# Thirteen GpSimd operations on a tile of their own in the end part of an attention and gMLP kernel

## The chip, the cores and the metric

The kernel runs on one core of a Trainium2 chip. The metric is the device time of one execution in microseconds. A core has five engines that run beside each other, each in the order of its own instructions: TensorE (PE, matmuls), VectorE (DVE), ScalarE (ACT), GpSimd (POOL) and SyncE (SP, which here only issues DMAs).

## The reference, cut to what matters

Attention with a threshold over 8 batches of 8 heads, 576 positions and 64 columns a head, followed by a gated MLP with a spatial projection (gMLP) over each batch. All inputs and the output are fp32.

```python
scores = q @ k.T / 8
scores = where(scores >= max(scores) - tau, scores, -1e9)
attn = exp(scores - max(scores)); attn /= sum(attn)
x = attn @ v                              # (8, 576, 512), the heads side by side
h = maximum(x @ w_in, 0)                  # (8, 576, 1024)
u, v = h[..., :512], h[..., 512:]
v_n = (v - mean(v)) / sqrt(var(v) + 1e-6)
v_s = w_spatial @ v_n + b_spatial         # over the 576 positions
out = (u * v_s) @ w_out                   # (8, 576, 512)
```

## The kernel before, in words

**Tiling.** The 64 heads go in 32 pairs. A pair has 576 rows of scores, four blocks of 128 and a rest of 64; the rests of two pairs share a block, so there are 144 steps. A step makes scores on PE (L830), their maximum on DVE (L859), a shift on POOL or DVE (L873, L869), the masked exponentials on ACT and DVE (L887, L890, L925, L909, L918), a transpose of the numerators by DMA (L930) and the product with v on PE (L505, L510), whose result DVE divides by the sums (L545, L548). When a batch has its x, the gMLP follows in blocks of 128 rows or columns: v (L641, L656), its norm (L675 to L708), u (L723, L728), the spatial product (L752, L757), the gate (L766, L769) and the output (L781, L792).

**The order.** It is written out by hand. ORDER holds one list of short tokens for each batch and `run_token` (L1111) turns a token into the instructions of one piece of work; nothing is reordered afterwards, so the order of the program is the order of each engine's own queue. A tile that one engine writes and another reads makes the reader wait; an instruction that waits holds up everything behind it on its engine.

**The end part.** After the eight lists comes LAST (L165), four short lists. LAST[1] ends the attention of the last two pairs and the output of batch 6; its last instructions on DVE and ACT are copies of output blocks (L792). Then `last_gmlp` (L941) does the gMLP of batch 7, in four parts between `yield`s:
- Part 1: 16 products for v (L955), the relu with ACT (L981, L984), the statistics on DVE (L961, L962). For chunk 3 ACT takes the sum, POOL makes the negative mean from it (L991) and ACT the squares (L995). POOL makes the reciprocal roots with a power: chunks 0 to 2 at once, chunks 3 and 4 later (both L965). The rest of v and the rest of batch 6's output are one bank (L641, L644), of which ACT takes one half here (L989).
- LAST[2]: u blocks 0 to 2 on PE (L723), which ACT evicts (L426).
- Part 2: shifts on DVE (L1004, L1007, L1012) and the norms, written to `vn`: chunks 0, 1 and 4 on DVE, 2 on POOL (all L970), 3 on ACT (L1010).
- LAST[3]: u block 3 and the rest of u (L723, L728).
- Part 3: ACT copies the other half of that bank (L1017), PE makes the spatial products (L1027: first the column blocks 0 and 1, chunk by chunk, then 2 and 3; then the rest, L1038), DVE gates (L1031, L1041), PE makes the output (L1048, L1059), ACT and DVE copy it out (L1050, L1064) and SP sends it (L1051, L1066); block 1 is sent by POOL's queue and one half of the rest by ACT's. The fourth part is empty.

PSUM has eight banks, which are used in turn, so a matmul can have to wait until the reader of a bank's former content is done. The third and fourth of the spatial products' banks had held L1017's half and the first block of u.

Of the kernel before, what the change touches and what calls it, by code (L numbers as in the profile page):

```python
# [9 lines left out]
F32 = mybir.dt.float32  # L10
# [5 lines left out]
ALU = mybir.AluOpType  # L16
# [172 lines left out]
def kernel(  # L189
# [17 lines left out]
    nc = tc.nc  # L207
    B, H, S, D = q.shape
# [5 lines left out]
    P = 128  # L214
    const = ctx.enter_context(tc.tile_pool(name="const", bufs=1))
# [28 lines left out]

    mhalf = const.tile([P, 1], F32, name="mhalf")
    zero = const.tile([P, 1], F32, name="zero")
    raised = const.tile([P, 2, 2], F32, name="raised")
    warm = const.tile([P, P], BF16, name="warm")

# [556 lines left out]
    def way(g):  # L806

        return WAYS[min(g // 18, len(WAYS) - 1)][g % 18]
# [34 lines left out]
    def turn_bank(g, eng):  # L843

        turned[g] = eng.nop()
        follow(turned[g], opened[g])
# [7 lines left out]
    def top(g, heads=slice(0, 2)):  # L854

        if g not in peak:
            peak[g] = small.tile([P, 2], F32, name="peak")
        for h in range(heads.start, heads.stop):
            nc.vector.tensor_tensor_reduce(  # L859
                out=e_ring[g % 3][:, h, :], in0=view(s_ring[g % 2], at[h], [[1, S]]),  # L860
                in1=zero.broadcast_to([P, S]), scale=1.0, scalar=float("-inf"),
                op0=ALU.add, op1=ALU.max, accum_out=peak[g][:, h:h + 1])

    def shift(g, engine):

        nm = negm[g] = small.tile([P, 2], F32, name="negm")
        down = -(scale if steps[g][1] == 4 else 1.0)
        if engine is nc.vector:
            engine.scalar_tensor_tensor(out=nm, in0=peak[g], scalar=down,  # L869
                                        in1=raised[:, 0 if way(g) == "a" else 1, :],  # L870
                                        op0=ALU.mult, op1=ALU.add)
        else:
            engine.tensor_scalar(out=nm, in0=peak[g], scalar1=down,  # L873
                                 scalar2=float(tau) + (0.0 if way(g) == "a" else half_step),
                                 op0=ALU.mult, op1=ALU.add)
# [6 lines left out]
    def spread(g, h):  # L882

        s = e_ring[g % 3][:, h, :]
        e, bias_ = e_ring[g % 3][:, h, :], negm[g][:, h:h + 1]
        if way(g) in "nrs":
            nc.scalar.activation(out=half_e(g)[0][:, h, :], in_=s, func=ACT.Exp,  # L887
                                 bias=bias_, scale=scale if steps[g][1] == 4 else 1.0)
        elif on_act(g):
            nc.scalar.activation(out=e, in_=s, func=ACT.Prelu, bias=bias_,  # L890
                                 scale=scale if steps[g][1] == 4 else 1.0, alpha=1e30)
        else:
            nc.scalar.activation(out=e, in_=s, func=ACT.Exp, bias=bias_)
# [217 lines left out]
    def run_token(tok, it):  # L1111

        name, _, d = tok.partition(":")
        on_vector[0] = name[0] == "d"
        name = name[on_vector[0]:]
        relay = nc.gpsimd
        if name[0] in "agv" and name[1] in "GB":
            relay = {"a": nc.scalar, "g": nc.gpsimd, "v": nc.vector}[name[0]]
            name = name[1:]
        b = it - int(d or 0)  # L1120
        if (name, b) in done or b < 0:
            return
        kind = name.rstrip("0123456789")
        a = [int(x) for x in name[len(kind):]] if kind not in "SGYMHKBEFZWCAT" else []
        g = 18 * b + int(name[len(kind):]) if kind in "SGYMHKBEFZWCAT" else 0
        if b >= B or g >= len(steps):
            return
        if kind in stepwise and way(g) not in stepwise[kind]:
            return
        i = 4 * b + a[0] if a else 0  # L1130
        m = 2 * b + a[0] if a else 0
        if kind in "SGYMHKEFBZWCAT":
            {"S": scores, "G": lambda g: turn_bank(g, relay), "Y": scores_end, "M": top, "E": lambda g: spread(g, 0),
             "F": lambda g: spread(g, 1), "H": lambda g: top(g, slice(0, 1)),
             "K": lambda g: top(g, slice(1, 2)), "B": lambda g: shift(g, relay), "Z": exps, "W": mask, "C": keep, "A": pick, "T": turn_p}[kind](g)
        elif kind in ("QA", "QB", "qa", "qb"):
            task("q", i, kind[1] in "Bb")[1 + (kind[0] == "q")]()
        elif kind in ("QR", "qr", "kd"):
            task("r", i)[1 + ("QR", "qr", "kd").index(kind)]()
        elif name == "sk1":  # L1140
            shape_qk(1, (1,))
        elif kind in ("sq", "sv"):
            (shape_qk if kind == "sq" else shape_v)(i)
        elif kind == "P":
            task("p", m, a[1])[0](a[2])
        elif kind in ("i", "p"):
            task("p", m, a[1])[1 + (kind == "p")]()
        elif kind in ("XP", "xp"):
            task("x", i, i == NPAIR - 1)[1 + (kind == "xp")]()
        elif kind in ("RP", "rp"):  # L1150
            task("t", m, a[1])[1 + (kind == "rp")]()
        elif kind in ("WS", "ws"):
            task("w", a[0])[1 + (kind == "ws")]()
        elif kind in ("X", "XR"):
            send_x(m, 4 if kind == "XR" or 2 * m in x_on_pe else 0, 5 if kind == "XR" else 9)
        elif kind == "L":
            load_of[b][a[0]]()
        elif kind[0] == "C":
            chores[kind[:2]][len(kind) == 3](a[0])
        elif kind == "OUT":  # L1160
            task("o", b, a[0])[3]() if a[0] < 4 else task("v", b + 1, 4)[6]()
        elif kind == "bv":
            task("v", b, a[0])[2](False)
        elif kind == "bs":
            task("v", b, a[0])[7]()
        elif kind == "ba":
            task("v", b, a[0])[8]()
        elif kind in ("n", "k", "N"):
            task("v", b, a[0])[3 + "nkN".index(kind)]()
        else:  # L1170
            task(kind[-1], b, a[0])[1 + (kind[0] == "e")]()
        done.add((name, b))
        on_vector[0] = False

    Z = B - 1
    with tc.manual_schedule():
        nc.vector.memset(warm, 1.0)
        for w in (1, 0):
            for h in range(2):
                load_first(w, h, (nc.sync, nc.scalar)[h])  # L1180
        for w in (0, 1):
            load_rest(0, w, 0, 2)()
        make_identity(nc, identf)
        clear()
        nc.vector.memset(zero, 0.0)
        nc.gpsimd.memset(raised[:, 0], float(tau))
        nc.gpsimd.memset(raised[:, 1], float(tau) + half_step)
        nc.vector.memset(ntau, -float(tau))
        nc.vector.memset(mhalf, -0.5)
        nc.scalar.activation(out=ctau, in_=ntau, func=ACT.Exp)  # L1190
        nc.vector.tensor_copy(out=identb, in_=identf)
        nc.vector.tensor_copy(out=identh, in_=identf)
        for w in (0, 1):
            load(1, 1, w)()
            load_rest(0, w, 2)()
        load(0, 2, 2)()
        for w in (2, 3):
            load_rest(0, w)()
        for _ in range(8):
            nc.tensor.matmul(out=next_bank().rearrange(  # L1200
                "p (a b) -> p a b", a=4), lhsT=warm,
                rhs=warm.unsqueeze(1).broadcast_to([P, 4, P]), start=True, stop=True)
        shape_first()
        first()
        clear_vn()
        shape_qk(1, (0,))
        load_of = [group_loads((b, 0)) + group_loads((b, 1)) for b in range(B)]
        for it in range(B):
            for tok in ORDER[min(it, len(ORDER) - 1)].split():
                run_token(tok, it)  # L1210

        for tok in LAST[0].split():
            run_token(tok, B)
        inner.close()
        wide.append(ctx.enter_context(tc.tile_pool(name="ps_t", bufs=6, space=PSUM,
                                                  reuse_waits="tile")))
        for tok in LAST[1].split():
            run_token(tok, B)
        rest = last_gmlp(Z)
        next(rest)  # L1220
        for tok in LAST[2].split():
            run_token(tok, B)
        next(rest)
        for tok in LAST[3].split():
            run_token(tok, B)
        next(rest)
        next(rest, None)


# [33 lines left out]
```

## Time and profile before

| | |
|---|---|
| Median of the runs | 429.72 us (2 runs, 429.71 to 429.73) |
| The profiled execution, its own time | 429.39 us |
| Its span in the profile | 427.6 us |
| Granted TensorE clock | 1.0 |
| Busy: PE, DVE, ACT, POOL | 405.0, 384.0, 386.1, 191.4 us |
| Traffic with HBM | 32.79 MB read, 9.44 MB written |

Times in the profile are microseconds from the start of the span. A row of the timeline gives the start, the duration, the engine, the line, the operation, what it writes and reads with shapes, and in brackets the idle time of the engine ahead of it and what ended that. Consecutive rows of the same kind are merged, with their number behind an x. A group row gives the number, the summed busy time and the mean in ns. PEld is TensorE's weight load, an engine name with a small q its instruction queue.

### The profile page before, as it was taken

What the parts mean: (1) busy time and instruction counts of PE and PEld (TensorE: products, weight loads), DVE (VectorE), ACT (ScalarE), POOL (GpSimd) and SP (SyncE); (2) the same over time, 40 slices, a digit from 0 to 9 for tenths busy, and PEclk for the clock granted to TensorE, in tenths of its full rate; (3) what the DMA queues carried; (4) which work ended last, traced back from release to release, by engine and by line L of the source; (5) the groups of instructions that cost most, each with busy time, mean ns of one, the idle gap of its engine ahead of it and who ended that gap; (6) DMA issues with size and microseconds to landing.
All of it is one profiled execution on the core that took longest, in us unless ns stands there. A gap on an engine that the chain in (4) does not pass through costs nothing.

```text
span 427.6 us, 13266 instructions
## 1 busy us (share of the span) xinstructions
PE 405.0 (95%) x4978; PEld 253.3 (59%) x5029; DVE 384.0 (90%) x1035; ACT 386.1 (90%) x567; POOL 191.4 (45%) x469
## 2 busy tenths in 40 slices
PE   8778978999999999999999999999999999999995
PEld 4456655566555675575665657656665666565642
DVE  6999989999899899989999999989999989999562
ACT  4999979999999999999999999999999999999362
POOL 2566437763246633554235631374233753255020
PEclk9999999999999999999999999999999999999999
DMA  7999999999999999998999989999989999989913
GB/s 196 288 280 182 263 273 227 168 182 195 239 265 171 214 213 188 204 210 227 214 165 280 211 165 252 217 221 210 236 138 229 228 214 206 160 150 214 180 57 117
DMA packets 224703, 88.18 MB, mean 206 GB/s; under 512 B 195648, under 2 KB 220352, under 8 KB 224640
## 3 DMA queue, kind: packets, MB, share of 16 engines
q1 hardware_dynamic: 224192, 86.75, 102.3%
q8 instruction: 39, 0.64, 0.6%
q10 hardware_dynamic: 368, 0.33, 0.2%
q0 software_dynamic: 80, 0.26, 0.2%
q14 instruction: 24, 0.20, 0.2%
HBM read 32.79 MB, written 9.44 MB: 99 GB/s over the span
## 4 chain that ended last, share of the span: by engine, by line
PE 62%; DVE 11%; ACT 9%; DMA 7%; issue 5%; POOL 3%; SPq 1%; POOLq 0%; DVEq 0%; ACTq 0%
PE s L830 25%; DVE e L859 7%; PE f L752 6%; DMA pT<-p 6%; PE f L448 5%; PE f L510 5%; PE f L723 4%; PE f L656 4%; ACT e L890 3%; PE f L781 3%; ACT e L887 2%; PE f L505 2%; ACT p L925 1%; DMA xT<-xn 1%; PE f L641 1%
## 5 line engine op out<-in xcount | busy, mean ns | idle before, releaser
L859 DVE CUSTOM_DVE_ANT_0 e<-s,zero 128x576 f32<-128x576 f32 x288 | 204.3, 752 | 5.8 <-PE s L830 1.4
L830 PE MATMUL s<-qkT 64*64 64x160 f32 (+1 forms) x2304 | 172.9, 413 | 4.5 <-DVE peak L859 3.7
L890 ACT ACTIVATE e<-e,negm 128x576 f32<-128x576 f32 x204 | 148.3, 766 | 4.8 <-PE s L830 2.3
L830 PEld LDWEIGHTS s<-qkT 64*64 64x64 f32 x2304 | 105.3, 132 | 53.2 <-issue 19.1
L925 ACT ACTIVATE p<-e 128x1152 f16<-128x1152 f32 x102 | 117.1, 1157 | 0.8
L873 POOL TENSOR_SCALAR negm<-peak 128x2 f32<-128x2 f32 x93 | 21.5, 231 | 133.3 <-DVE peak L859 89.7
L887 ACT ACTIVATE e<-e,negm 128x576 f16<-128x576 f32 x84 | 62.4, 767 | 2.0 <-POOL negm L873 1.3
L510 PE MATMUL f<-v,pT 128*128 128x65 bf16 x984 | 44.6, 194 | 0.0
L510 PEld LDWEIGHTS <-pT 128*128 128x128 f16 x1024 | 41.9, 98 | 2.4 <-issue 0.6
L918 DVE TENSOR_TENSOR p<-e 128x576 int32<-128x576 int32 x42 | 34.4, 822 | 0.5
L752 PE MATMUL f<-wsT,vn 128*128 128x512 bf16 x121 | 31.9, 380 | 0.9 <-DVE qkT L424 0.2
L505 PE MATMUL f<-v,pT 128*128 128x130 bf16 x123 | 27.2, 221 | 4.0 <-DMA pT<-p 3.9
L333 POOL CAST v<-vl 128x512 bf16<-128x512 f32 x32 | 21.3, 666 | 18.6 <-PE s L830 17.5
L708 POOL TENSOR_SCALAR vn<-vrel,rs,nm 128x512 bf16<-128x512 f32 (+1 forms) x35 | 27.9, 798 | 3.6
L723 PE MATMUL f<-xT,w_in 128*128 128x512 bf16 x102 | 28.5, 380 | 1.0 <-ACT qkT L430 0.3
L656 PE MATMUL f<-w_in,xT 128*128 128x512 bf16 x98 | 27.0, 380 | 1.4 <-DMA xT<-xn 0.3
L548 DVE TENSOR_TENSOR xn<-f,r 128x384 bf16<-128x384 f32 x46 | 25.2, 554 | 0.7
L781 PE MATMUL f<-w_o,gT 128*128 128x512 bf16 x94 | 25.1, 379 | 0.4
L859 DVE DVE_READ_ACCUMULATOR2_ANT peak<- 128x1 f32 x288 | 23.9, 83 | 0.0
L306 POOL COPY qn<-ql 128x512 f32<-128x512 f32 x31 | 19.7, 636 | 5.9 <-DMA ql<-in_q_dram 2.7
L752 PEld LDWEIGHTS <-vn 128*128 128x128 bf16 x140 | 12.8, 98 | 15.5 <-issue 3.1
L448 PE MATMUL f<-identf,kn 128*128 128x128 f32 x124 | 19.8, 282 | 2.2 <-DVE qkT L424 1.5
(175 smaller groups left out, 560.2 us busy)
## 6 DMA issues: line engine op xcount, KB each, us to landing
vl<-in_v_dram SPq DMA_DIRECT2D x16, 512.0 KB, 5.2
ql<-in_q_dram SPq DMA_DIRECT2D x15, 512.0 KB, 5.5
kl<-in_k_dram SPq DMA_DIRECT2D x15, 512.0 KB, 5.7
out_dram<-oo SPq DMA_DIRECT2D x12, 512.0 KB, 4.2
pT<-p SPq DMA_TRANSPOSE x141, 4.4
uT<-in_moe_w_in_dram SPq DMA_DIRECT2D x3, 512.0 KB, 6.4
uT<-in_moe_w_spatial_dram SPq DMA_DIRECT2D x2, 576.0 KB, 6.8
vx<-in_v_dram SPq DMA_DIRECT2D x16, 64.0 KB, 3.8
```

Of the source, the lines that this page charges most:

```text
L448: nc.tensor.transpose(out=t[:, c * P:(c + 1) * P], in_=nat[i][which][:, c, :], identity=identf)
L505: nc.tensor.matmul(out=t[:, at:at + 130], lhsT=pt[:, 4, rows], rhs=vt[:, 4:6, :].rearrange("p b d -> p (b d)"), start=True, stop=False)
L510: nc.tensor.matmul(out=t[:, at + 65 * h:at + 65 * h + 65], lhsT=pt[:, 5 * h + j, rows], rhs=vt[:, 6 * h + j, :], start=False, stop=(h == 1 ...
L656: nc.tensor.matmul(out=t, lhsT=x_of(b, f, slice(c * P, (c + 1) * P)), rhs=w_in[:, f, 512:1024], start=(f == 0), stop=(f == 3))
L723: nc.tensor.matmul(out=t, lhsT=w_in[:, m, f * P:(f + 1) * P], rhs=x_of(b, m, slice(0, 512)), start=(m == 0), stop=(m == 3))
L752: nc.tensor.matmul(out=t, lhsT=vn[:, c, f * P:(f + 1) * P], rhs=wsT[:, c, 0:512], start=(c == 0), stop=(c == 4))
L781: nc.tensor.matmul(out=t[:n], lhsT=gs[b][:, f, c * P:c * P + n], rhs=w_o[:, f, :], start=(f == 0), stop=(f == 3))
L830: made.append(nc.tensor.matmul(out=s_ring[g % 2][halves[k], at[h] + lo:at[h] + hi], lhsT=qks[n][halves[h], 0, m:m + 64], rhs=qks[n][halves ...
L859: nc.vector.tensor_tensor_reduce(out=e_ring[g % 3][:, h, :], in0=view(s_ring[g % 2], at[h], [[1, S]]), in1=zero.broadcast_to([P, S]), scal ...
L887: nc.scalar.activation(out=half_e(g)[0][:, h, :], in_=s, func=ACT.Exp, bias=bias_, scale=scale if steps[g][1] == 4 else 1.0)
L890: nc.scalar.activation(out=e, in_=s, func=ACT.Prelu, bias=bias_, scale=scale if steps[g][1] == 4 else 1.0, alpha=1e30)
L925: nc.scalar.activation(out=numerators(g), in_=e_ring[g % 3].rearrange("p h s -> p (h s)"), func=ACT.Exp)
```

## The change

Two tiles are added, a column of ones and a tile `trial` of 128x576 fp32. DVE fills the column at the start, and `trial` after LAST[1]. Nine operations on POOL follow, ahead of `last_gmlp`, and four more behind its third part. Each reads `trial` and writes it in place; scalars are numbers or the columns `zero` and `one`. One of the thirteen is a tensor_tensor with the column `zero` repeated over the free dimension, the others are tensor_scalar with one or two operations. Nothing else reads `trial`.

```diff
@@ -244,6 +244,8 @@
     mhalf = const.tile([P, 1], F32, name="mhalf")
     zero = const.tile([P, 1], F32, name="zero")
+    one = const.tile([P, 1], F32, name="one")
+    trial = const.tile([P, S], F32, name="trial")
     raised = const.tile([P, 2, 2], F32, name="raised")
@@ -1183,6 +1185,7 @@
         nc.vector.memset(zero, 0.0)
+        nc.vector.memset(one, 1.0)
@@ -1216,6 +1219,16 @@
         for tok in LAST[1].split():
             run_token(tok, B)
+        nc.vector.memset(trial, 2.0 ** -6)
+        nc.gpsimd.tensor_scalar(out=trial, in0=trial, scalar1=zero, scalar2=2.0 ** -3, op0=ALU.subtract, op1=ALU.mult)
+        nc.gpsimd.tensor_scalar(out=trial, in0=trial, scalar1=zero, scalar2=2.0 ** -3, op0=ALU.add, op1=ALU.mult)
+        nc.gpsimd.tensor_scalar(out=trial, in0=trial, scalar1=one, scalar2=zero, op0=ALU.mult, op1=ALU.add)
+        nc.gpsimd.tensor_scalar(out=trial, in0=trial, scalar1=zero, scalar2=None, op0=ALU.subtract)
+        nc.gpsimd.tensor_scalar(out=trial, in0=trial, scalar1=2.0 ** -120, scalar2=None, op0=ALU.mult)
+        nc.gpsimd.tensor_scalar(out=trial, in0=trial, scalar1=one, scalar2=zero, op0=ALU.mult, op1=ALU.add)
+        nc.gpsimd.tensor_tensor(out=trial, in0=trial, in1=zero.broadcast_to([P, S]), op=ALU.subtract)
+        nc.gpsimd.tensor_scalar(out=trial, in0=trial, scalar1=zero, scalar2=one, op0=ALU.add, op1=ALU.mult)
+        nc.gpsimd.tensor_scalar(out=trial, in0=trial, scalar1=one, scalar2=None, op0=ALU.mult)
         rest = last_gmlp(Z)
         next(rest)
         for tok in LAST[2].split():
@@ -1224,6 +1237,10 @@
         for tok in LAST[3].split():
             run_token(tok, B)
         next(rest)
+        nc.gpsimd.tensor_scalar(out=trial, in0=trial, scalar1=zero, scalar2=one, op0=ALU.subtract, op1=ALU.mult)
+        nc.gpsimd.tensor_scalar(out=trial, in0=trial, scalar1=2.0, scalar2=zero, op0=ALU.mult, op1=ALU.add)
+        nc.gpsimd.tensor_scalar(out=trial, in0=trial, scalar1=zero, scalar2=2.0, op0=ALU.is_ge, op1=ALU.mult)
+        nc.gpsimd.tensor_scalar(out=trial, in0=trial, scalar1=zero, scalar2=None, op0=ALU.add)
         next(rest, None)
```

## The prediction

> **What bounds the kernel now.** The page of the profile comes first: TensorE, VectorE and ScalarE are busy for 90% or more of the span, GpSimd (POOL) for less than half, and in the last tenth of the span POOL is nearly empty.
>
> ```profile
> span 427.6 us, 13266 instructions
> PE 405.0 (95%) x4978; PEld 253.3 (59%) x5029; DVE 384.0 (90%) x1035; ACT 386.1 (90%) x567; POOL 191.4 (45%) x469
> POOL 2566437763246633554235631374233753255020
> ```
>
> A share over the whole span says nothing of a stage, so the chain of work that ended last, cut to the last 35 us, is next. It runs over TensorE without a gap: products for the last batch (L955), ends and u (L641, L723, L728), the spatial products (L1027, L1038), the output products (L1048, L1059).
>
> ```profile
> 413.64 0.47 PE t L728 x16
> 414.11 2.16 PE t L1027 x10
> 416.26 2.16 PE f L1027 x10
> 418.42 0.58 PE t L1038 x20
> ...
> 423.01 0.05 PE f L1059
> ```
>
> So PE sets the end, and POOL's results cost nothing as long as they stand ready when PE comes to them. How much they have to spare is in the timeline of the same stage (start, duration, engine, line, operation, in brackets the idle time before it).
>
> ```profile
> 405.70 0.68 DVE L792 COPY vl<-f 128x512 f32<-128x512 f32 x1
> 406.34 0.06 DVE L948 MEMSET var<- 128x5 f32 x1
> 408.47 0.69 DVE L961 BATCH_NORM_STATS2 st<-vrel 128x6 f32<-128x512 f32 x1 [2.05 <-ACT vrel L981]
> 410.15 0.19 POOL L991 TENSOR_SCALAR nmean<-sm 128x1 f32<-128x1 f32 x1 [15.82 <-ACT vrel L984]
> 410.62 0.71 ACT L995 ACTIVATE sq<-vrel,nmean 128x512 bf16<-128x512 f32 x1
> 411.23 0.19 ACT L995 ACTIVATION_READ_ACCUMULATOR sq<-vrel,nmean 128x1 f32 x1
> 411.26 0.87 POOL L965 TENSOR_TENSOR rstd<-var,mhalf 128x3 f32<-128x3 f32 x1 [0.92 <-DVE var L985]
> 411.32 0.58 ACT L426 ACTIVATE uT<-f 128x512 bf16<-128x512 f32 x1
> 411.95 0.60 ACT L426 ACTIVATE uT<-t 128x512 bf16<-128x512 f32 x1
> 412.07 0.14 DVE L1000 TENSOR_SCALAR var<-ss 128x1 f32<-128x1 f32 x1
> 412.16 0.16 DVE L1004 SCALAR_TENSOR_TENSOR shift<-mvs,rstd 128x3 f32<-128x3 f32 x1
> 412.29 0.70 POOL L965 TENSOR_TENSOR rstd<-var,mhalf 128x2 f32<-128x2 f32 x1 [0.16 <-DVE var L1000]
> 412.36 0.55 DVE L970 TENSOR_SCALAR vn<-vrel,rstd,shift 128x512 bf16<-128x512 f32 x1
> 412.99 0.77 POOL L970 TENSOR_SCALAR vn<-vrel,rstd,shift 128x512 bf16<-128x512 f32 x1
> 413.10 0.94 DVE L970 TENSOR_SCALAR vn<-vrel,rstd,shift 128x512 bf16<-128x512 f32 x1
> 413.31 0.80 ACT L1010 ACTIVATE vn<-vrel,shift,rstd 128x512 bf16<-128x512 f32 x1
> 414.12 0.54 DVE L970 TENSOR_SCALAR vn<-o,rstd,shift 64x512 bf16<-64x512 f32 x1
> 414.88 0.58 ACT L1017 COPY kl<-f 64x512 f32<-64x512 f32 x1
> 421.65 0.78 POOL L1051 DMA_DIRECT2D out_dram<-ql  x1 [7.90 <-ACT ql L1050]
> ```
>
> POOL has two idle stretches here: 15.82 us before L991 and 7.90 us before its one DMA. But the first ends in the norms of the last batch, and these run POOL, ACT, DVE, POOL, DVE, PE in turn. Chunk 0 of vn is ready at 412.91 and PE turns to L1027 at 414.11; chunk 1 is ready at 414.04 and is wanted at 414.54. The spare time is about a microsecond at most.
>
> **The change, part by part.** Nothing is removed and nothing is moved. Added are a memset of a 128x1 column at the start, a memset of the 128x576 tile on DVE, nine operations on POOL behind it, and four more on POOL behind the output stage.
>
> The small memset (128x1) costs DVE no more than the five columns of L948, 0.06 us; DVE waits for the first loads behind it, which hides it, and without that cover it costs the 0.06. Taken as 0.
>
> The large memset stands in DVE's order behind the copy of 405.70, which ends at 406.38. Its price comes from two memsets of other sizes:
>
> ```profile
> L269 DVE MEMSET vn<- 64x512 bf16 x2 | 1.0, 485 | 0.2 <-issue 0.2
> L1177 DVE MEMSET warm<- 128x128 bf16 x1 | 0.2, 165 | 0.8 <-PEq L1244 0.8
> ```
>
> That is (485 - 165) / 384 = 0.83 ns for an element and 0.54 us for 576. On DVE it lies in the 2.05 us of idle time before L961; uncovered it would cost 0.54. On POOL it matters at once, because the first operation waits for it: 406.38 + 0.54 + 0.08 for the handover gives 407.00. So of POOL's 15.82 us of idle time only the last 3.15 can be used: the operations start 12.6 us after the idle time does.
>
> The nine operations work in place, each on the result of the one before. All but one are TENSOR_SCALAR, one is TENSOR_TENSOR with a repeated column. No row has this size or these combinations, so the nearest rows of POOL are these (first two lines: one source line with its minimum, median and maximum; then groups with a mean; then two copies in time order):
>
> ```profile
> L708 POOL TENSOR_SCALAR vn<-vrel,rs,nm x35: 761/767/1202, 77.3 to 389.4; 128x512 bf16<-128x512 f32 x28, 64x512 bf16<-64x512 f32 x7
> L703 POOL TENSOR_SCALAR nm<-mv,rs x28: 252/259/585, 76.9 to 389.0; 128x1 f32<-128x1 f32 x22, 64x1 f32<-64x1 f32 x6
> ...
> L394 POOL TENSOR_TENSOR bias<-bias,wsb 128x5 f32<-128x5 f32 x2 | 0.4, 198 | 0.2
> ...
> 100.54 0.61 POOL L306 COPY qn<-ql 128x512 f32<-128x512 f32 x1
> 101.10 0.61 POOL L306 COPY kn<-kl 128x512 f32<-128x512 f32 x1
> ...
> 389.02 0.26 POOL L703 TENSOR_SCALAR nm<-mv,rs 128x1 f32<-128x1 f32 x1
> 389.38 0.77 POOL L708 TENSOR_SCALAR vn<-vrel,rs,nm 128x512 bf16<-128x512 f32 x1
> ```
>
> From 259 ns for one column and 767 for 512 follows 0.99 ns an element, so 0.83 us for 576; a dependent operation follows 0.10 behind the one before it (389.28 to 389.38). That makes 0.93 from start to start. The low end is a plain copy, 0.56 from start to start, 0.63 at 576. The high end is L708's slowest, 1.20, which at 576 with the gap is 1.45. I take 0.93 for each of the eight, because L708 is the same kind of instruction. The TENSOR_TENSOR took 0.198 at five columns (L394), against 0.19 for one column (L991; 0.185 within its rounding), so at most 3.3 ns an element: its price lies between 0.63 (as the copy) and an estimated 2.1 (0.19 + 1.9 at 576, and the gap). I take 1.4, the middle. Sum: 8 x 0.93 + 1.4 = 8.84 us, and the ninth ends at T = 415.84; with the low prices (9 x 0.63) at 412.7, with the high ones (8 x 1.45 + 2.1) at 420.7.
>
> Who is queued behind them: L991, both L965, POOL's L970 and POOL's DMA L1051, all in POOL's order. L991 would have started at 410.15 and now starts at T + 0.1. What follows, with the durations above:
> - L991 ends at T + 0.29. ACT's square starts at T + 0.33 and its sum is read at T + 1.13 (0.80 as from 410.62 to 411.42). Queued behind the square on ACT are three evictions of u, and behind these L1010 (vn chunk 3).
> - POOL's first L965 runs from T + 0.39 to T + 1.26, beside the square. DVE's L1000 stands ahead of L1004 in DVE's order, so DVE comes to the shifts at T + 1.36, and chunk 0 is written at T + 2.1.
> - The second L965 ends at T + 2.12; DVE's chunk 1 is ready at T + 3.2 and chunk 4 at T + 3.8, at the distances that they have behind it now.
> - ACT: 0.70 to the first eviction, 3 x 0.63 for the evictions (two of them waited for PE before, now all three are ready), then L1010 at T + 2.92, and from there 2.15 to the end of L1017 (413.31 to 415.46): T + 5.07.
> - PE: chunk 1 at T + 3.2 and four chunks of 0.43 end the first ten of L1027 at T + 4.9. The next ten write the bank that L1017 reads, so they start at T + 5.10, where they started at 416.26. Everything behind that moves as one.
>
> The end is late by T + 5.10 - 416.26 = T - 411.16. For T = 415.84 that is **4.7 us**. The low prices give 1.5, the high ones 9.5; nothing in the edit takes work away, so below nothing is excluded.
>
> The last four operations follow POOL's DMA. On the old time scale that DMA issue ends at 422.43, and four of 0.93 end at about 426.2. The end then waits for the last output DMA:
>
> ```profile
> out_dram<-ql ACTq DMA_DIRECT2D x1, 64.0 KB, 2.8
> ...
> 423.55 0.55 ACTq L1066 DMA_DIRECT2D out_dram<-ql  x1
> ```
>
> It lands at 423.55 + 2.8 = 426.35. The four are hidden, with some 0.15 us to spare; at 1.45 each they end at 428.3 and cost 1.9. I take 0.
>
> Sum: the profiled execution took 429.39 (span 427.6), and with 4.7 it takes 434.1; the runs shown lie 0.33 above that execution (429.72), so 434.4.
>
> **The rivals.**
> *Everything is hidden: not slower.* The break-even is T = 411.16, so nine operations in 4.16 us, 0.46 us each. That needs POOL to stream these forms faster than its plain copy (0.63 at this size); no row does. The time would be 429.7. The same time would come out if the dead results made the operations vanish, for which I see no reason.
> [...]
>
> *TensorE's clock falls.* By the working above PE has nothing to do from 414.11 to about 418.0 (T + 2.1), 3.9 us. The one place where the granted clock fell is the end of the span (columns: window, its length, busy time of five engines, granted clock, DMA share, GB/s):
>
> ```profile
> 427.20:427.40 0.20, 0.00 (x0) 0.00 (x0) 0.00 (x0) 0.00 (x0) 0.00 (x0) 1.00 0.00 0
> 427.40:427.60 0.20, 0.00 (x0) 0.00 (x0) 0.00 (x0) 0.00 (x0) 0.00 (x0) 0.60 0.00 0
> ```
>
> That is 4.3 us after the last matmul (423.06). 3.9 is just short of it, which speaks against a fall here. If it fell to 0.60, the 8.5 us of PE work still open (6.8 from 416.26 to 423.06, and 1.7 of the first ten) would take up to 5.7 more; with about half of it at that clock, 2.9: 437.3.
> [...]
>
> *Some form is far dearer than L708.* POOL's power took 0.87 for three columns and 0.70 for two (L965), 0.17 a column, so single operations can be slow by orders. Against it: the added ones only add, subtract, multiply and compare. If three of the first nine took 3 us, T and the end move by 6.2: 440.6.
>
> *The last four set the end*, at 1.45 each: 434.4 + 1.9 = 436.3.
>
> **How the numbers follow.** Forecast 0.57; last four 0.12; clock 0.12; a dear form 0.12; all hidden 0.07. The range goes from the low prices, 429.7 + 1.5 = 431.2, to the high ones, 429.7 + 9.5 = 439.2; that leaves out the hidden case and most of the dear form. A difference of 2% is 8.6 us, about what a measurement of this kernel can tell from no change: 438.3 is passed by most of the dear forms and by a part of the clock case, 0.13 together; faster by 2% needs work to disappear, 0.01; within, 0.86.
>
> **What would show it.** In the profile after: the memset on DVE at about 406.4, POOL's first added operation near 407.0, the ninth ending near 415.8, L991 right behind it; ACT's wait ahead of L995 and PE's wait ahead of L1027 (near 4 us, put down to vn) in place of none; the second ten of L1027 behind L1017; the last four under the landing of the last DMA. The chain would pass over POOL. It is wrong if L991 keeps its 410.15, if PE does not wait ahead of L1027, if PE's clock drops there, or if the last instruction of POOL ends the span.

## The result, and the profile after

The changed kernel takes 443.23 us (442.58 to 443.87, 2 runs) against 429.72, a ratio of 1.0314 with a 95% interval of 1.025 to 1.0379: slower by over 2%, and above the range. The forecast was 434.4. The profiled execution took 443.87 with a span of 442.0, which is 14.4 more than the span of before.

The first view is the timeline of POOL in the changed kernel (start, duration, line, shapes, idle time before; the lines of the old code stand two or more higher than before: L991 is now L993, L965 L967, L970 L972, L1010 L1012, L1017 L1019, L1027 L1029).

```profile
408.06 2.22 POOL L1223 TENSOR_SCALAR trial<-trial,zero 128x576 f32<-128x576 f32 x1 [12.79 <-DVE mvs L951]
410.38 0.74 POOL L1224 TENSOR_SCALAR trial<-trial,zero 128x576 f32<-128x576 f32 x1
411.22 0.82 POOL L1225 TENSOR_SCALAR trial<-trial,one,zero 128x576 f32<-128x576 f32 x1
412.13 1.73 POOL L1226 TENSOR_SCALAR trial<-trial,zero 128x576 f32<-128x576 f32 x1
413.95 1.66 POOL L1227 TENSOR_SCALAR trial<-trial 128x576 f32<-128x576 f32 x1
415.71 0.82 POOL L1228 TENSOR_SCALAR trial<-trial,one,zero 128x576 f32<-128x576 f32 x1
416.61 1.15 POOL L1229 TENSOR_TENSOR trial<-trial,zero 128x576 f32<-128x576 f32 x1
417.87 0.81 POOL L1230 TENSOR_SCALAR trial<-trial,zero,one 128x576 f32<-128x576 f32 x1
418.78 1.72 POOL L1231 TENSOR_SCALAR trial<-trial,one 128x576 f32<-128x576 f32 x1
420.46 0.19 POOL L993 TENSOR_SCALAR nmean<-sm 128x1 f32<-128x1 f32 x1
...
433.79 2.29 POOL L1240 TENSOR_SCALAR trial<-trial,zero,one 128x576 f32<-128x576 f32 x1
436.19 0.74 POOL L1241 TENSOR_SCALAR trial<-trial,zero 128x576 f32<-128x576 f32 x1
437.04 2.21 POOL L1242 TENSOR_SCALAR trial<-trial,zero 128x576 f32<-128x576 f32 x1
439.35 1.74 POOL L1243 TENSOR_SCALAR trial<-trial,zero 128x576 f32<-128x576 f32 x1
```

Operations of one size and one opcode (TENSOR_SCALAR) cost between 0.74 and 2.29 us. Then the chain of work that ended last, which now passes over POOL:

```profile
418.78 1.72 POOL trial L1231
420.50 0.17 POOL nmean L993
...
423.58 3.58 PE t L1029 x8
427.17 2.52 PE f L1029 x10
429.69 0.58 PE t L1040 x20
```

And the busy time in stretches of the end part (length; PE, PEld, DVE, ACT, POOL busy; granted clock; DMA share; GB/s):

```profile
415.00:422.40 7.40, 0.00 (x1) 0.01 (x1) 0.77 (x3) 1.71 (x5) 6.74 (x8) 0.67 0.00 0
422.40:427.17 4.77, 4.63 (x11) 1.46 (x12) 1.92 (x5) 2.60 (x6) 0.84 (x2) 0.50 0.13 27
...
417.40:417.60 0.20, 0.00 (x0) 0.00 (x0) 0.00 (x0) 0.00 (x0) 0.20 (x1) 0.84 0.00 0
417.60:417.80 0.20, 0.00 (x0) 0.00 (x0) 0.00 (x0) 0.00 (x0) 0.15 (x1) 0.50 0.00 0
...
427.60:427.80 0.20, 0.20 (x2) 0.00 (x0) 0.20 (x1) 0.00 (x0) 0.00 (x0) 0.56 0.00 0
427.80:428.00 0.20, 0.20 (x2) 0.10 (x1) 0.20 (x1) 0.00 (x0) 0.00 (x0) 1.00 0.00 0
```

PE has nothing to do for 7.4 us, its clock falls to half in that time and stays there for the first half of the spatial products. The 14.4 us of the span come apart as follows:
- **0.9** lie ahead of the end part: DVE's copy of 405.70 now starts at 406.60. Run e8 below shows no such cost of the two tiles, and in e5, the same kernel once more, the first of the nine starts at 407.17 and not at 408.06, so it is scatter between executions.
- **8.15** are the nine (by working out): the first ten of L1029 would have ended at 423.58 + 8 x 0.216 = 425.31 at full clock, where they ended at 416.26 + 0.9.
- **2.2** are the clock: these eight took 3.58 in place of 1.73, and the ten behind them 2.52 in place of 2.16.
- **3.1** are the last four: from the last DMA issue to the end it is 442.0 - 434.81 = 7.19, and it was 427.6 - 423.55 = 4.05. The waits of SP's queue at the end (us in total, times, longest) are for the last output DMA, as before (2.3 there too), and for POOL's last operation:

```profile
SPq L1275 <- POOL trial L1243: 3.1, 1, 3.1
SPq L1275 <- DMA out_dram<-ql: 2.3, 1, 2.3
```

### The profile page after: what moved, and what is told of

It is laid out like the page before. It is cut to its first block, busy times and chain, and to the rows that moved or that the text cites. A ratio compares the mean times of both kernels' runs of the same rounds, so it can differ in the third digit from the quotient of the medians.

```text
span 442.0 us, 13332 instructions
## 1 busy us (share of the span) xinstructions
PE 412.1 (93%) x5029; PEld 254.3 (58%) x5029; DVE 384.5 (87%) x1037; ACT 385.7 (87%) x567; POOL 210.3 (48%) x482
## 4 chain that ended last, share of the span: by engine, by line
PE 63%; DVE 11%; POOL 7%; ACT 6%; DMA 6%; issue 5%; POOLq 0%; SPq 0%; DVEq 0%; ACTq 0%
PE s L832 25%; DVE e L861 7%; PE f L754 6%; PE f L512 5%; PE f L450 5%; PE f L725 5%; DMA pT<-p 4%; PE f L658 4%; PE f L783 3%; ACT e L892 2%; PE f L507 2%; DMA xT<-xn 1%; PE f L469 1%; ACT p L927 1%; ACT e L889 1%
## 5 line engine op out<-in xcount | busy, mean ns | idle before, releaser
L920 DVE TENSOR_TENSOR p<-e 128x576 int32<-128x576 int32 x42 | 34.3, 821 | 0.4
L754 PE MATMUL f<-wsT,vn 128*128 128x512 bf16 x135 | 32.8, 380 | 0.2 <-DVE qkT L426 0.2
L725 PE MATMUL f<-xT,w_in 128*128 128x512 bf16 x116 | 29.4, 380 | 0.4 <-ACT qkT L432 0.3
L658 PE MATMUL f<-w_in,xT 128*128 128x512 bf16 x112 | 28.1, 380 | 0.5 <-DVE qkT L426 0.2
```

Of the source, the lines that this page charges most:

```text
L658: nc.tensor.matmul(out=t, lhsT=x_of(b, f, slice(c * P, (c + 1) * P)), rhs=w_in[:, f, 512:1024], start=(f == 0), stop=(f == 3))
L725: nc.tensor.matmul(out=t, lhsT=w_in[:, m, f * P:(f + 1) * P], rhs=x_of(b, m, slice(0, 512)), start=(m == 0), stop=(m == 3))
L754: nc.tensor.matmul(out=t, lhsT=vn[:, c, f * P:(f + 1) * P], rhs=wsT[:, c, 0:512], start=(c == 0), stop=(c == 4))
```

## The experiments

The theory: POOL's price for a tensor_scalar goes by its operations, some pairs are fast and all else is slow; the nine then hold up the norms, the idle time lowers PE's clock, and the last four set the end. The rivals: the slow ones are slow by circumstance (first after a pause, other engines at work), or by the values that they work on; the slow spatial products come from late chunks and not from the clock; work on POOL slows VectorE. In these runs the kernel before took 430.3 to 430.8 us (medians), and single runs of it lay between 428.0 and 432.6.

**e1, the forms alone.** The thirteen are taken out and 23 operations stand behind the output, on an otherwise idle core.

```diff
         next(rest, None)
+        nc.gpsimd.tensor_scalar(out=trial, in0=trial, scalar1=1.0, scalar2=0.0, op0=ALU.mult, op1=ALU.add)
+        nc.gpsimd.tensor_scalar(out=trial, in0=trial, scalar1=1.0, scalar2=None, op0=ALU.mult)
...
```

> The nine and the four are taken out; 23 operations on the added tile stand behind everything else, so POOL runs them alone after the output: ten further combinations, a copy, two TENSOR_TENSOR, and three forms at 64 and 256 columns. The time itself says nothing here; the rows do. Theory 'form' (a fast way only for two operations that are both add or mult): two-operation add/mult forms 0.74 to 0.82 us whatever the scalars are; one operation 1.65 to 1.75; a first operation subtract, is_ge or max 2.2 to 2.3. The slope per element (576 against 64 columns) is about 1.0 ns for the fast form and 2.7 to 3.5 for the slow ones. Rival 'circumstance' (the first operation after a pause, or DVE and ACT working beside it, makes it slow): all forms take 0.7 to 0.9 when POOL is alone and runs one after the other.

One line's instruction each (minimum, median and maximum in ns of the one execution):

```profile
L1232 POOL TENSOR_SCALAR trial<-trial x1: 680/680/680, 422.3 to 422.3; 128x576 f32<-128x576 f32 x1
L1233 POOL TENSOR_SCALAR trial<-trial x1: 1676/1676/1676, 423.0 to 423.0; 128x576 f32<-128x576 f32 x1
L1234 POOL TENSOR_SCALAR trial<-trial,one,zero x1: 821/821/821, 424.8 to 424.8; 128x576 f32<-128x576 f32 x1
L1237 POOL TENSOR_SCALAR trial<-trial,zero,one x1: 2304/2304/2304, 429.3 to 429.3; 128x576 f32<-128x576 f32 x1
L1241 POOL TENSOR_SCALAR trial<-trial x1: 673/673/673, 437.2 to 437.2; 128x576 f32<-128x576 f32 x1
L1242 POOL TENSOR_SCALAR trial<-trial x1: 2144/2144/2144, 438.0 to 438.0; 128x576 f32<-128x576 f32 x1
L1246 POOL COPY trial<-trial x1: 660/660/660, 447.0 to 447.0; 128x576 f32<-128x576 f32 x1
L1249 POOL TENSOR_SCALAR trial<-trial x1: 242/242/242, 450.2 to 450.2; 128x64 f32<-128x64 f32 x1
L1250 POOL TENSOR_SCALAR trial<-trial x1: 376/376/376, 450.5 to 450.5; 128x64 f32<-128x64 f32 x1
```

In this order: mult then add with two numbers; a single mult; mult then add with two columns; subtract then mult with two columns; mult twice; add twice; a copy; mult then add, and a single mult, on 64 columns. The prices are the same as in the changed kernel, on an idle core and anywhere in the row of operations, so circumstance falls. Values are no cause either: the fifth of the nine takes `trial` from 2^-12 to 2^-132 by arithmetic, below the smallest normal fp32 number, and the same forms cost the same ahead of it and behind it (0.82 and 0.82; 1.73 and 1.72). The theory holds but for one point: I had "two operations that are both add or mult", and add twice is slow (2.14). The pairs seen fast are mult with add in either order (0.68; add then mult in e10, 0.68), and mult twice (0.67). A column for a number adds 0.07 us (0.821 against 0.680 with two). Per element the fast form costs (680 - 242) / 512 = 0.86 ns, the single operation (1676 - 376) / 512 = 2.5 ns.
The fixed part is 0.19 us by these rows (0.242 less 64 x 0.86 ns). L708 follows from them too: 512 x 0.86 ns, the 0.19 and two columns at 0.07 make 0.77, and its median is 0.767.
It is not the number of operations that decides: one costs 1.65, and two cost 0.68 or 2.15.

**e10, more forms.** As e1, with fourteen others, some on a 16-bit tile whose content is no longer needed.

```diff
         next(rest, None)
...
+        nc.gpsimd.tensor_scalar(out=p_ring[0][:, 0:S], in0=trial, scalar1=1.0, scalar2=None, op0=ALU.mult)
...
+        nc.gpsimd.tensor_scalar(out=trial, in0=trial, scalar1=0.0, scalar2=None, op0=ALU.add)
```

> Again with all thirteen out and fourteen other operations alone behind the output; only the rows count. By the rows so far two operations are fast when they are mult and add in either order or mult twice, and add twice is slow, so: add then mult 0.68, subtract twice and mult then max 2.15. New: the result in 16 bits, and both in 16 bits. If the slow way is a way per operation and not per type, one operation stays at 1.65 and mult then add at 0.68 whatever the types; if types decide, the 16-bit ones differ. Half the partitions: no shorter, 1.65. One column: both forms 0.2 to 0.3. A single max or add: 1.65.

```profile
421.69 0.68 POOL L1232 TENSOR_SCALAR trial<-trial 128x576 f32<-128x576 f32 x1
422.45 2.16 POOL L1233 TENSOR_SCALAR trial<-trial 128x576 f32<-128x576 f32 x1
...
429.42 0.67 POOL L1237 TENSOR_SCALAR p<-p 128x576 f16<-128x576 f16 x1
430.18 1.65 POOL L1238 TENSOR_SCALAR p<-p 128x576 f16<-128x576 f16 x1
...
436.23 1.64 POOL L1241 TENSOR_SCALAR trial<-trial 64x576 f32<-64x576 f32 x1
...
440.27 1.66 POOL L1245 TENSOR_SCALAR trial<-trial 128x576 f32<-128x576 f32 x1
```

In this order: add then mult; subtract twice; mult then add, and a single mult, both on 16 bits; a single mult on 64 partitions; a single add. All as expected: the 16-bit type is without effect on both forms (0.67 and 1.65, with fp32 0.68 and 1.65 to 1.68 in e1), half the partitions on the single mult (1.64), the only form tried there.

**e2, the same thirteen as fast pairs**, in the same places.

```diff
-        nc.gpsimd.tensor_scalar(out=trial, in0=trial, scalar1=one, scalar2=None, op0=ALU.mult)
+        nc.gpsimd.tensor_scalar(out=trial, in0=trial, scalar1=one, scalar2=0.0, op0=ALU.mult, op1=ALU.add)
...
-        nc.gpsimd.tensor_scalar(out=trial, in0=trial, scalar1=zero, scalar2=2.0, op0=ALU.is_ge, op1=ALU.mult)
+        nc.gpsimd.tensor_scalar(out=trial, in0=trial, scalar1=zero, scalar2=2.0, op0=ALU.add, op1=ALU.mult)
```

> All thirteen stay, in the same places, but each tensor_scalar is written with two operations out of add and mult (the single ones get a second one that changes nothing, subtract and is_ge become add). Theory 'form': the nine take 8 x 0.9 + 1.25 = 8.4 us, end near 415.5 on the time scale of before, the end part is 4.4 us late, PE idles about 3.5 us, and the last four (3.6 us) end under the last DMA: 434.1, up to 436 if the clock still falls. Rival 'circumstance': nothing changes, 443.

435.25 us, ratio 1.0126 (1.0088 to 1.0164). Seven of the thirteen were rewritten, with an operation more in four of them, and by the ratios 8 us are gone. This is nearly the kernel that I had predicted, and it shows the rest of the working near its forecast prices: the nine take 8.0 us (406.59 to 414.61), the last four end at 430.86 (430.12 + 0.74), ahead of the landing of the last DMA at about 431.36 (428.56 + 2.8), and cost nothing: from that DMA's issue to the end it is 4.04 us, and 4.05 before. Yet the clock falls here too (1.00 up to 417.8, 0.50 from 418.0 on), with PE idle for 2.98 us only:

```profile
416.51 0.60 PE L1029 MATMUL t<-wsT,vn 128*128 128x512 bf16 x2 [2.98 <-DVE vn L972]
417.69 3.43 PE L1029 MATMUL t<-wsT,vn 128*128 128x512 bf16 x8 [0.57 <-DVE shift L1014]
```

**e3, the nine alone, and e4, the four alone** (the memset stays in both).

```diff
-        nc.gpsimd.tensor_scalar(out=trial, in0=trial, scalar1=zero, scalar2=one, op0=ALU.subtract, op1=ALU.mult)
...
```

> The last four are taken out, the first nine stay. If the last four set the end of the changed kernel, they cost 3.1 us: 440.1. If they are hidden, as I predicted, 443.2 stays.

> The first nine are taken out (with the memset left), the last four stay. If the delay of the norms and the end wait add up, this costs 3.1 us over the kernel before: 432.9. If the last four cost something only because the rest was late, 429.7.

e3: 439.82, ratio 1.0237 (1.0196 to 1.0278), 10.2 us at the ratio. e4: 432.75, ratio 1.0057 (1.0037 to 1.0077), 2.5 us with 1.6 to 3.3. Both as expected, and together 12.7, while e5 (the changed kernel again) has 12.5 over the same kernel before: the two places add up.

**e5, the changed kernel again**, for e6 to be set beside it; no edit.

> The changed kernel once more, so that the next ones have it on the same chip: 13.5 us over the kernel before (443 to 444).

443.26, ratio 1.0291 (1.0251 to 1.0331).

**e6, PE kept at work in the idle time.**

```diff
         gated = {}
+        held = gated[0] = bank()
+        for _ in range(32):
+            nc.tensor.matmul(out=held, lhsT=identb, rhs=w_o[:, 0, :], start=True, stop=True)
```

> The changed kernel with 32 more matmuls of 512 columns (0.216 us each, 6.9 us) on PE, written into the bank that the first spatial product overwrites, so that PE is not idle from 415.0 to about 421.9 of the changed kernel. Nothing else is changed and the thirteen stay where they are. Theory 'clock' (TensorE's clock falls to half in the idle time and the first fourteen or so spatial products run at half speed): the granted clock stays at 1.00 there, the first eight matmuls behind the wait take 1.73 us in place of 3.58, and the time falls by 1.9 to 2.2 us against the changed kernel. Rival 'data' (these matmuls are slow because the chunks of vn come late one after the other): no change in time, since the chunks come as late as before.

440.87, ratio 1.0236 (1.0206 to 1.0267): 2.4 us less than e5 by the medians, but the two intervals overlap, so the total alone does not show it; the rows do. POOL's operations take what they took in the changed kernel, and the granted clock, 0.50 in e5 from 419.4 to 426.0, is 1.00 here over the first spatial products. The rows are three of PE's timeline in e6, a stretch of e6 with the clock (third number from the end), and the eight products in the chain of e6 and in that of e5:

```profile
414.61 7.07 PE L1027 MATMUL t<-w_o,identb 128*128 128x512 bf16 x32
422.18 0.60 PE L1032 MATMUL t<-wsT,vn 128*128 128x512 bf16 x2 [0.50 <-DVE vn L972]
423.36 1.90 PE L1032 MATMUL t<-wsT,vn 128*128 128x512 bf16 x8 [0.57 <-DVE shift L1014]
...
421.68:425.30 3.62, 2.54 (x11) 1.01 (x12) 2.19 (x6) 3.11 (x7) 1.34 (x2) 1.00 0.00 0
...
423.37 1.89 PE t L1032 x8
...
422.71 3.57 PE t L1029 x8
```

The chunks come at the same distances (e2 has the pause of 0.57 ahead of the eight too), and the eight take 1.89 where e5 has 3.57. That is the clock and not the data: 1.7 us of the span behind the first spatial product are gone (422.18 to 439.8, against 421.51 to 440.8 in e5), though PE does more work.

**e7, the nine earlier**, in their dear forms, where POOL's idle time begins. (Here and in e9 the diff shows the moved lines at their new place alone.)

```diff
+        nc.vector.memset(trial, 2.0 ** -6)
...
         for tok in LAST[0].split():
             run_token(tok, B)
+        nc.gpsimd.tensor_scalar(out=trial, in0=trial, scalar1=zero, scalar2=2.0 ** -3, op0=ALU.subtract, op1=ALU.mult)
...
         inner.close()
```

> The nine, in the same dear forms (12.5 us), start some 12 us earlier: the large memset is done at the start of the kernel and the nine stand behind the first list of the end part, where POOL's idle time begins; the four are left as they are. Theory 'place' (what the nine cost is only that they begin 12.6 us late and then hold up the norms): they end near 407, ahead of the first operation of the norms, so only the last four cost something: 2.4 to 3.1 us over the kernel before (432.5 to 433.5). Rival 'contention' (thirteen slow operations on POOL slow VectorE's work on the last attention steps): longer than that by over 1 us, with DVE's rows between 395 and 406 longer.

433.26, ratio 1.0066 (1.0038 to 1.0094), 2.8 us at the ratio: what is left is the last four, as in e4. The nine run from 395.1 to 407.6, and POOL still waits 3.43 us ahead of the norms. On VectorE one operation beside them is longer (L911 at 395.37, 0.79 us, where L909 of before took 0.46 at 394.69); L920, which reads what it writes, starts 0.33 us later for it. Further on it is not to be seen: PE's wait for the transposed block behind ends 8.17 us after the start of L911 (403.54), and 8.13 after it in e8 (394.84 to 402.97), where POOL has none of the nine. In the profile before, L909 takes 0.42 to 0.46 us wherever POOL is idle beside it, and up to 0.81 where POOL is at work. So contention is there in a row, and none is clear in the time.

**e8, the tiles and memsets alone.**

```diff
-        nc.gpsimd.tensor_scalar(out=trial, in0=trial, scalar1=zero, scalar2=2.0 ** -3, op0=ALU.subtract, op1=ALU.mult)
...
-        nc.gpsimd.tensor_scalar(out=trial, in0=trial, scalar1=zero, scalar2=None, op0=ALU.add)
```

> The two tiles and the two memsets without the thirteen operations. I expect the time of the kernel before, within 0.3 us: the large memset lies in DVE's idle time. If the shift of everything by 0.9 us that the changed kernel shows ahead of the end part comes from the place of the tiles in memory, this is 0.9 us slower; if that is the ordinary scatter between executions, it is not.

430.36, ratio 0.9987 (0.9965 to 1.0008): they cost 0.3 us at the most.

**e9, all thirteen in hidden places**: the nine as in e7, the four between POOL's share of the norms and its DMA.

```diff
         next(rest)
+        nc.gpsimd.tensor_scalar(out=trial, in0=trial, scalar1=zero, scalar2=one, op0=ALU.subtract, op1=ALU.mult)
...
         for tok in LAST[3].split():
             run_token(tok, B)
```

> All thirteen in the same dear forms, none taken out: the nine behind the first list of the end part as in the run before, the four (2.3 + 0.75 + 2.2 + 1.75 and gaps, 7.3 us) behind POOL's chunk of the norms, in the 7.9 us before its DMA. Theory 'place': about 20 us of work on POOL cost at most 0.5 us (the four end within half a microsecond of the DMA's turn). Rival 'contention' (POOL at work through the spatial products and gates slows VectorE's products, or its DMA is late and its block lands last): 1 to 3 us slower than the kernel before.

430.5, ratio 1.0 (0.9973 to 1.0027), so 1.2 us either way is open. The same work in the same forms has no cost clear of the noise where nobody waits for POOL:

```profile
405.68 1.72 POOL L1226 TENSOR_SCALAR trial<-trial,one 128x576 f32<-128x576 f32 x1
410.79 0.19 POOL L993 TENSOR_SCALAR nmean<-sm 128x1 f32<-128x1 f32 x1 [3.40 <-ACT vrel L986]
...
414.46 2.45 POOL L1237 TENSOR_SCALAR trial<-trial,zero,one 128x576 f32<-128x576 f32 x1
...
420.17 1.74 POOL L1240 TENSOR_SCALAR trial<-trial,zero 128x576 f32<-128x576 f32 x1
422.38 0.82 POOL L1053 DMA_DIRECT2D out_dram<-ql  x1 [0.46 <-ACT ql L1052]
```

## Why the prediction was wrong

The forecast was 4.7 us more and the measurement 13.5. The terms of the sum that were off make up the difference: the nine 8.15 in place of 4.7, the last four 3.1 in place of 0, the clock 2.2 in place of 0. The step that failed is the price of an operation. By itself it would not have left the range: T was 419.6 on the old time scale (420.50 less 0.9), under the high end of 420.7, and 429.7 + 8.15 is 437.9. But the range was worked out from the nine alone, with the last four and the clock at 0 at both of its ends, and by its own working neither could be 0 at the high prices. Two of the signs that the prediction had named for being wrong came: PE's clock dropped ahead of the spatial products, and POOL's last instruction ended the span.

**Right: the place.** The wait for the large memset (0.538 us, forecast 0.54), the start right behind it, L991 at the back of the nine, and the chain from there over ACT, POOL and DVE to PE. By the formula T - 411.16, with T = 420.50 less the 0.9 of scatter, the delay without the clock is 8.4; it was 8.15. One of its terms was too long: two evictions of u on ACT took 1.07 together, so L1019 was done at 425.01, before the first ten spatial products ended (427.17, or 425.31 at full clock), and it was these and not the shared bank that set the start of the next.

**Wrong: the price of an operation.** "I take 0.93 for each of the eight, because L708 is the same kind of instruction." L708 multiplies and then adds, one of the fast pairs; for those the price was right (0.74 to 0.82 with 0.83 forecast, before the gap). Of the eight, three have a single operation (1.66 to 1.73) and one begins with a subtract (2.22). Together the nine took 12.4 us and not 8.84; the TENSOR_TENSOR, 1.4 in the sum, took 1.15 and a gap. The rival of the dear form was stated, but as something improbable and with the power as its only row; and the range's high end, L708's slowest 1.20 carried to 1.45, was the scatter of one form and no bound on another. That the nine still came in under its sum is luck: four operations stood above 1.45 and four below. The low end took the plain copy for the cheapest operation; a single operation costs 2.5 times the copy (1.66 and 0.66 in e1).

**Wrong: the last four.** Hidden at 0.93 each, with 0.15 us to spare; they took 2.29, 0.74, 2.21 and 1.74, and the end waited 3.1 us for them. This is the same price again; e2 and e4 show it, 0 with the fast pairs and 2.5 with the dear forms.

**Wrong: the clock.** I set 3.9 us of idle time against the one fall that the profile before showed, 4.3 us behind the last matmul, and took that for a threshold. In the changed kernel it fell 2.5 us behind the last matmul (415.0, fall at about 417.54), and in e2 at about 417.88, when PE was at work again. In e5, the same kernel, it fell at about 419.31, 5.2 us behind the last matmul (414.11). So it is not a fixed time counted from the last matmul, and the 4.3 was no threshold. The 0.60 of before was the mean of a slice in which the fall lay; the low clock is 0.50 (there too, from 427.45 on). The rival's price of 2.9 was near the 2.2 measured by luck: it took the clock too high and about half of 8.5 us of work to run at it, where 2.2 us of it on the chain did. e2 shows that with the prices that I had forecast this rival could come true as well.

Three causes that I had as separate rivals at 0.12 each came together. They are not independent: dear operations stand in both places, and they lengthen the idle time in which the clock can fall.

## What to carry to other kernels

The price of a POOL operation is read from a row with the same operations, not with the same opcode; alone on 128x576 (e1, e10) a mult with an add took 0.68 us (0.82 with two columns), a single operation 1.65 to 1.73, two and a half times that, and a pair with a subtract, a compare, a max or two adds 2.14 to 2.30, three times. A single mult or add, or a subtract of a number, can be rewritten as a mult with an add, which buys that back (in e2 1.73 and 2.22 became 0.74); a compare or a max cannot. Idle time of an engine is of use only from the moment at which its input is there and until the first result on which another engine's chain hangs (in the changed kernel the first 12.79 us of POOL's went in the wait for the memset); e9 put the same 20 us of work into POOL's idle time with no cost clear of the noise. A wait that leaves PE idle for some 3 us can cost the clock on top (2.98 us in e2 did), so it is to be priced with the half-speed matmuls behind it (eight took 3.43 us there, and 1.90 at full clock in e6).

## What the runs showed of the hardware

The low clock came in stretches of one, two and three times one length. In the changed kernel it is low from 417.54 to 427.78 (from the shares in the rows above), 10.2 us. In e2 it is low from 417.88 to 421.30, 3.4 us, a third of that (first two rows below). In e5, the changed kernel again, it is low from 419.31 to 426.14, 6.8 us, two thirds (last two rows):

```profile
417.80:418.00 0.20, 0.20 (x2) 0.07 (x1) 0.20 (x1) 0.20 (x1) 0.00 (x0) 0.72 0.00 0
421.20:421.40 0.20, 0.20 (x2) 0.07 (x1) 0.20 (x1) 0.00 (x0) 0.00 (x0) 0.74 0.00 0
...
419.20:419.40 0.20, 0.00 (x0) 0.00 (x0) 0.00 (x0) 0.00 (x0) 0.20 (x1) 0.77 0.00 0
426.00:426.20 0.20, 0.20 (x2) 0.11 (x1) 0.20 (x1) 0.00 (x0) 0.00 (x0) 0.66 0.01 0
```

In the changed kernel's profile it is low once more, under the attention, from 59.14 to 62.55, 3.4 us. PE need not be empty ahead of a fall: in e2 the 3.4 us ahead of it hold two matmuls (416.51) and the start of a third.

In the 3.41 us that ended at the fall PE had 0.80 us of matmuls in e2, 0.87 in the changed kernel (414.13 to 417.54), 1.57 at its fall of 59.14, and none in e5. In e5 the 3.41 us before those (412.48 to 415.90) held 1.63, and the clock did not fall at their end. But the amount of work alone does not decide: in e5 PE had no matmul from 414.11 on, and the clock held until 419.31, 5.2 us. What decides was not shown.

A type of fp32 or fp16 made no difference to POOL's price for the two forms tried (0.68 us in fp32 and 0.67 in fp16 for mult then add, 1.65 to 1.68 and 1.65 for a single mult; e1, e10), nor did 64 or 128 partitions for a single mult (1.64, and 1.65 to 1.68); the number of columns (0.24 us at 64 and 0.68 at 576 for mult then add) and the operations did. Why add twice is slow and mult twice fast stays open.
